# Float64 weights converted two tiles at a time, with larger shared homes and a new order of steps

## The chip, the cores and the metric

The kernel runs on one core of one Trainium2 chip. The metric is device time in microseconds (us) for one launch; lower is better.

## The reference, cut to what matters

Two attentions through a small "pack" of 32 tokens for each of 8 batches and 8 heads, and then a feed-forward layer over all 4608 tokens. The weights `w_in` and `w_out` come in float64, everything else in float32.

```python
def sm_attn(qq, kk, vv):
    s = scale * np.matmul(qq, kk.transpose(0, 1, 3, 2))
    s = s - np.max(s, axis=-1, keepdims=True)
    a = np.exp(s)
    a = a / (np.sum(a, axis=-1, keepdims=True) + 1e-09)
    return np.matmul(a, vv)
p_packed = sm_attn(p, k, v)                 # 32 packed tokens a head
out = sm_attn(q, p_packed, p_packed)        # (8, 8, 576, 64)
x = out.transpose(0, 2, 1, 3).reshape(4608, 512)
h = x @ w_in                                # 512 -> 2048
g = np.maximum(h, 0.0) + alpha * np.minimum(h, 0.0)
y = g @ w_out                               # 2048 -> 512
```

## The kernel before

Everything up to `h` is folded: for each batch the packed tokens are multiplied with `w_in` (tiles `pw`), and `first(k, f)` makes one 128 x 288 piece of `h` from `pw` and the attention weights `a` of half a batch `k` and the block `f` of 128 hidden columns. It then forms `neg`, `ps_h`, `gh` and `gl` on ScalarE (ACT) and VectorE (DVE): `g` split into a high and a low part. `second(k, f)` multiplies these with the block `f` of `w_out` (twelve matmuls, lines 693 to 695) into four accumulators. `order` lists the (k, f) pairs; I call one entry a step. Step i's `first` is issued together with step i-2's `second`. Batches 0 and 1 go in sweeps over a few blocks f at a time, so that a step needs only what has been converted by then; from batch 2 on all 16 blocks go in one sweep.

Before a weight can be used its float64 words are turned into float32 words on the chip by `convert`: DMA of the raw 64-bit words into `wraw`; ACT takes the magnitude of the high words (line 121, read with a step of two words) and scales the low words by 2^-29 (line 123); DVE clamps (125), shifts and masks (128), puts the sign back (132, whose first source is again every second word of `wraw`), and adds the low word as an exact 32-bit addition on 16-bit limbs (137 for `w_in`, 139 for `w_out`; shown in rows as CUSTOM_DVE or ISA, with twice the element count since the elements are 16-bit). For `w_out` ACT then rounds to the high part (141) and DVE subtracts it (142). One call converts one tile of 128 x 512; there are 16 tiles of `w_in` and 16 of `w_out`, and so 32 calls. `w_in` is also written back to DRAM (`w_whole`) for later batches.

The homes of `w_out` (tags `wo0` to `wo15`, 4 KB a partition each) serve as landing places before their own block is there: for the first k, v and q tiles, for the packed tokens `pt0`, and, five of them in turn (`SPARE`), for the raw words.

The order of the work is set in two ways. A fixed string, `'zzzzzzzzPzzzzozPzzoz'`, interleaves the attention of batch 0 (z), the conversions of the first block of `w_in` (P, `packed_w_fine`) and of `w_out` (o). After it a table of numbers, `plan`, says from which step on, and how often a step, each generator is advanced. The scheduler of the framework then sets the final order on each engine; every engine works through its own queue in that order, and SP is the queue that issues nearly all DMAs.

Of the kernel before, what the change touches and what calls it, by code (L numbers as in the profile page):

```python
# [28 lines left out]
def pack_attention_ffn_kernel(  # L29
# [54 lines left out]

    s1f = const.tile([P, NP, 2, 64], F32, name="s1f")
    ptf = const.tile([P, NP, 2, 64], F32, name="ptf")
    pt0 = const.tile([P, NP, 2, 64], F32, name="pt0", tag=f"wo{NF - 1}")
# [4 lines left out]
    s1 = const.tile([P, NP, 2, 64], F32R, name="s1")  # L92
    p2 = const.tile([P, NP, 2, 64], F32R, name="p2")
# [4 lines left out]
    nc.gpsimd.tensor_copy(out=ii[64:128], in_=ident[64:128, 64:128])  # L98
    for t in (ptf, pt0, fv(s1), fv(p2)):
        nc.gpsimd.memset(t, 0.0)  # L100
    wo_t = {}


    XF = 1

    def convert(src, raw, place, whole=None, room=None):
# [32 lines left out]
        nc.vector.tensor_tensor(out=bits, in0=bits, in1=low, op=ALU.add)  # L139
        hi, lo = place()  # L140
        nc.scalar.copy(out=hi, in_=mag)
        nc.vector.tensor_tensor(out=lo, in0=mag, in1=fv(hi), op=ALU.subtract)

    def new_raw(f=0):

        if f in left:
            left.remove(f)
            n = f
        elif f == NF - 1:
            n = f  # L150
        else:
            n = left.pop(0)
            left.append(n)
        return const.tile([P, 512], U64, name=f"wraw{n}", tag=f"wo{n}")

    SPARE = 5
    left = list(range(NF - 1 - SPARE, NF - 1))

    def convert_w_out(f):
        def place():  # L160
            wo_t[f] = const.tile([P, 2, DM], F32R, name=f"wo{f}", tag=f"wo{f}")
            return wo_t[f][:, 0, :], wo_t[f][:, 1, :]

        return convert(w_out[f * P : (f + 1) * P, :], new_raw(f), place)


    def load_x(src, b, pr):
        if b == 0 and (src is kT or pr == NP - 1):
            n = pr if src is kT else 2 * NP
            raw = const.tile([P, S], F32, name=f"xraw{n}", tag=f"wo{n}")  # L170
# [12 lines left out]
    def load_v(b, pr):  # L183
        if b == 0:
            raw = const.tile([P, KT, P], F32, name=f"vraw{pr}", tag=f"wo{NP + pr}")
# [43 lines left out]
    def attention(b, tp, exact=False):  # L229
# [6 lines left out]
        ts = slice(2 * tp, 2 * tp + 2)  # L236
        st1 = [s1f[:, pr, pr % 2] for pr in range(NP)] if exact else [s1[:, pr] for pr in range(NP)]
        st2 = [ptf[:, pr, b % 2] if exact else p2[:, pr] for pr in range(NP)]
# [7 lines left out]
        k1 = load_x(kT, b, pr1)  # L246
        yield
        if tp == 0:
            for r in range(2):
# [88 lines left out]
        yield  # L338
        c = sm.tile([P, 2, P], F32, name="c", tag="c", bufs=2)

        def pack(i, vs):
# [150 lines left out]
    def new_w32():  # L492
        return win.tile([P, 512], F32, name="w32", tag="w")

    def convert_w_in(j, pr, place, whole=None):
        src = w_in[pr * P : (pr + 1) * P, j * 512 : (j + 1) * 512]
        return convert(src, new_raw(), place, whole)

    def packed_w_fine(j):


        def get(f):
            cols = slice((4 * j + f) * P, (4 * j + f) * P + P)
# [18 lines left out]
        for f in range(4):  # L522
            ps = ps_m.tile([P, 512], F32, name="ps_m", tag="m")
            for pr in range(NP):
# [11 lines left out]
            if f == 3:  # L536
                done.update(("w", 0, j, pr) for pr in range(NP))
            if f < 2:
                ws.append(get(f + 2))
            yield  # L540

    def packed_w_first(j):

        ws = []
        for pr in range(NP):
            w = new_w32()
            drain(convert_w_in(j, pr, None, lambda: w))
            nc.sync.dma_start(out=w_whole[j, pr], in_=w)
            ws.append(w)
            if pr < 2:  # L550
                yield
                continue
            if pr == 2:
                gen = packed_w_whole(j, ws)
                next(gen)
                next(gen)
                yield
                continue
            next(gen)
            next(gen)  # L560
            yield

    def packed_w_two(bs, units, fresh):


        def get(j, pr):
            w = new_w32()
            if fresh:
                drain(convert_w_in(j, pr, None, lambda: w))
                nc.sync.dma_start(out=w_whole[j, pr], in_=w)  # L570
            else:
                nc.sync.dma_start(out=w, in_=w_whole[j, pr])
            return w

        for got in ahead(get, units):
            if got is None:
                yield
                continue
            (j, pr), w = got
            if pr == 0:  # L580
# [61 lines left out]
    def first(k, f):  # L642
# [132 lines left out]
    wf = packed_w_fine(0)  # L775
    wo = w_out_steps(range(NF))
# [8 lines left out]
    A2 = (24, 28, 35, 38, 50)  # L785
    AG = (0, 5, 11, 15, 24)
    plan = [(0, wf, 1), (WO[0], slower(WO[1], WO[2], wo), 1), (W1, packed_w_first(1), 1)]
    plan += [(0, gen, -2) for gen in later]
    plan += [(AT1[0], attention(1, 0, True), AT1[2]), (AT1[1], attention(1, 1, True), AT1[2])]
# [56 lines left out]
```

## Time and profile before

| | us |
|---|---|
| median of 3 runs (lowest, highest) | 795.83 (794.82, 796.27) |
| the profiled execution | 795.78 |
| its span, first to last instruction | 793.9 |
| outside the span | 1.9 |
| PE busy | 768.2 (97%) |
| ACT busy | 544.4 (69%) |
| DVE busy | 478.2 (60%) |
| POOL busy | 348.3 (44%) |

PE is TensorE's matmuls, PEld its weight loads. A busy share is a mean over the whole span; the kernel has a head, in which weights are converted and the first attentions run, and a long even part after it, and the shares differ between them. In rows with a time in front the first number is the start in us from the span's start, the second the duration. Durations of neighbouring instructions of one engine overlap a little, so the cost of one to its queue is the distance between two starts.

### The profile page before, as it was taken

How to read it: one execution, taken by the hardware profiler on the slowest of the kernel's cores; microseconds unless marked ns; L12 is line 12 of the kernel's file. 1: busy time of each engine (PE TensorE's matmuls, PEld its weight loads, DVE VectorE, ACT ScalarE, POOL GpSimd, SP SyncE). 2: the span in 40 equal slices, each digit the busy share in tenths (PEclk: the TensorE clock that was granted, in tenths of full speed). 3: DMA queues.
4: the chain of work that ended last, by engine and by line, in shares of the span. 5: the costliest groups of instructions: out<-in, count | busy, mean ns of one | idle time of the engine just before them, and what ended most of it. 6: DMA issues, size and time to landing. Idle time of an engine off the chain costs nothing.

```text
span 793.9 us, 15186 instructions
## 1 busy us (share of the span) xinstructions
PE 768.2 (97%) x5360; PEld 724.8 (91%) x5360; DVE 478.2 (60%) x1080; ACT 544.4 (69%) x1260; POOL 348.3 (44%) x327
## 2 busy tenths in 40 slices
PE   5699998999999999999999999999999999999997
PEld 4467677999899899999999999999999999999997
DVE  3999889678766335758565345757663344444443
ACT  5778789776667986767667876768678644444443
POOL 2102305654566764666664335667543222222220
PEclk9999999999999999999999999999999999999999
DMA  9887653211443981312223651222037000000000
GB/s 332 309 273 257 212 181 124 79 53 53 155 128 105 315 300 49 109 46 76 63 78 128 230 170 46 76 68 70 1 98 248 30 31 2 31 1 31 5 26 31
DMA packets 59611, 91.69 MB, mean 115 GB/s; under 512 B 5264, under 2 KB 37008, under 8 KB 59536
## 3 DMA queue, kind: packets, MB, share of 16 engines
q1 hardware_dynamic: 59248, 90.66, 35.1%
q8 instruction: 42, 0.69, 0.3%
q14 instruction: 33, 0.27, 0.1%
q10 hardware_dynamic: 288, 0.07, 0.0%
HBM read 68.69 MB, written 22.02 MB: 114 GB/s over the span
## 4 chain that ended last, share of the span: by engine, by line
PE 85%; DVE 5%; ACT 4%; DMA 4%; issue 1%; POOL 0%; SPq 0%; ACTq 0%; DVEq 0%
PE acc L693 16%; PE acc L694 16%; PE acc L695 16%; PE ps_h L663 7%; PE ps_h L665 7%; PE ps_h L664 7%; PE ps_h L651 3%; PE ps_m L350 2%; PE ps_m L587 2%; PE ps_m L216 1%; PE ps_m L217 1%; PE ps_m L622 1%; PE ps_m L624 1%; PE ps_m L623 1%; DMA w_whole<-w 1%
## 5 line engine op out<-in xcount | busy, mean ns | idle before, releaser
L693 PE MATMUL acc<-gh,wo 128*128 128x288 f32 x1024 | 287.2, 300 | 1.6 <-ACT gh L675 1.5
L694 PE MATMUL acc<-gh,wo 128*128 128x288 f32 x1024 | 282.5, 295 | 0.0
L639 POOL TENSOR_TENSOR pwl<-pw,pwh 128x512 fp32r<-128x512 f32 x112 | 146.4, 1308 | 218.7 <-ACT pwh L638 187.1
L670 DVE SCALAR_TENSOR_TENSOR ps_h<-neg,nal,ps_h 128x288 f32<-128x288 f32 x256 | 132.6, 519 | 151.6 <-ACT neg L669 150.9
L693 PEld LDWEIGHTS acc<-gh,wo 128*128 128x128 f32 x1024 | 192.2, 188 | 9.6 <-ACT gh L675 6.0
L695 PE MATMUL acc<-gl,wo 128*128 128x288 f32 x1024 | 199.4, 298 | 0.0
L694 PEld LDWEIGHTS acc<-gh,wo 128*128 128x128 f32 x1024 | 192.3, 188 | 1.9 <-issue 0.7
L676 DVE TENSOR_TENSOR gl<-ps_h,gh 128x288 fp32r<-128x288 f32 x256 | 116.2, 455 | 88.7 <-ACT gh L675 85.9
L695 PEld LDWEIGHTS acc<-gl,wo 128*128 128x128 f32 x1024 | 157.5, 188 | 4.2 <-issue 1.6
L675 ACT CAST gh<-ps_h 128x288 fp32r<-128x288 f32 x256 | 101.9, 400 | 72.9 <-DVE ps_h L670 70.8
L669 ACT ACTIVATE neg<-ps_h 128x288 f32<-128x288 f32 x256 | 104.8, 409 | 49.2 <-PE ps_h L665 39.0
L663 PE MATMUL ps_h<-a_h,pwh 128*128 128x288 f32 x448 | 133.4, 298 | 0.6 <-DVE gl L676 0.6
L665 PE MATMUL ps_h<-a_h,pwl 128*128 128x288 f32 x448 | 132.2, 295 | 0.0
L664 PE MATMUL ps_h<-a_l,pwh 128*128 128x288 f32 x448 | 132.2, 295 | 0.0
L638 ACT CAST pwh<-pw 128x512 fp32r<-128x512 f32 x112 | 69.4, 620 | 57.9 <-PE ps_h L664 56.1
L180 POOL TENSOR_TENSOR xl<-xraw,xh 128x576 fp32r<-128x576 f32 x48 | 69.8, 1455 | 71.8 <-ACT xh L179 67.8
L663 PEld LDWEIGHTS ps_h<-a_h,pwh 128*128 128x128 f32 x448 | 84.1, 188 | 1.6 <-DVE gl L676 1.1
L664 PEld LDWEIGHTS ps_h<-a_l,pwh 128*128 128x128 f32 x448 | 84.2, 188 | 1.0 <-issue 0.5
L665 PEld LDWEIGHTS ps_h<-a_h,pwl 128*128 128x128 f32 x448 | 84.1, 188 | 0.2
L627 ACT COPY pw<-ps_m 64x512 f32<-64x512 f32 x96 | 55.8, 581 | 5.8 <-PE ps_m L624 4.2
L309 POOL TENSOR_TENSOR vs<-vraw,vs 128x640 fp32r<-128x640 f32 x24 | 37.7, 1571 | 24.2 <-ACT vs L308 22.2
L219 ACT COPY lo<-ps_m 64x288 f32<-64x288 f32 x96 | 37.6, 396 | 10.1 <-PE ps_m L217 8.5
(130 smaller groups left out, 990.7 us busy)
## 6 DMA issues: line engine op xcount, KB each, us to landing
w<-w_split SPq DMA_DIRECT2D x32, 512.0 KB, 4.0
xraw<-in_kT SPq DMA_DIRECT2D x32, 288.0 KB, 3.0
xraw<-in_qT SPq DMA_DIRECT2D x32, 288.0 KB, 3.0
outT<-ot SPq DMA_DIRECT2D x64, 144.0 KB, 2.0
vraw<-in_v SPq DMA_DIRECT2D x32, 256.0 KB, 2.9
wraw<-in_w_in SPq DMA_DIRECT2D x16, 512.0 KB, 5.0
wraw<-in_w_out SPq DMA_DIRECT2D x16, 512.0 KB, 4.9
w_split<-w SPq DMA_DIRECT2D x16, 512.0 KB, 3.5
```

What stands on the lines that cost most here:

```text
L180: nc.gpsimd.tensor_tensor(out=xl, in0=raw, in1=fv(xh), op=ALU.subtract)
L639: nc.gpsimd.tensor_tensor(out=tl, in0=src, in1=fv(th), op=ALU.subtract)
L663: nc.tensor.matmul(ps[:, :HS], th[:, i, fs], a_h[:, i, tok], start=hi, stop=False)
L664: nc.tensor.matmul(ps[:, :HS], th[:, i, fs], a_l[:, i, tok], start=False, stop=False)
L665: nc.tensor.matmul(ps[:, :HS], tl[:, i, fs], a_h[:, i, tok], start=False, stop=lo)
L669: nc.scalar.activation(out=neg, in_=x, func=AF.Relu, scale=-1.0)
L670: nc.vector.scalar_tensor_tensor(out=x, in0=neg, scalar=nal[:, f : f + 1], in1=x, op0=ALU.mult, op1=ALU.add)
L675: nc.scalar.copy(out=gh, in_=x)
L676: nc.vector.tensor_tensor(out=gl, in0=x, in1=fv(gh), op=ALU.subtract)
L693: nc.tensor.matmul(acc[o][:, :HS], wo_t[f][:, 0, os_], gh, start=begin, stop=False)
L694: nc.tensor.matmul(acc[o][:, :HS], wo_t[f][:, 1, os_], gh, start=False, stop=False)
L695: nc.tensor.matmul(acc[o][:, :HS], wo_t[f][:, 0, os_], gl, start=False, stop=end)
```

## The change

Each call of `convert` now handles two tiles, 128 x 1024. The four (for `w_out` five) DVE instructions and the two (three) ACT instructions of a call have twice the width, and there are 16 calls in place of 32. For `w_in` the magnitude is made directly in the result tile `w32` (now 128 x 1024, four KB) and for `w_out` in one `mag` buffer of its own. The low word is scaled in place in `wraw`, so the exact addition reads it there, in every second 32-bit word, where it was read before from a dense tile `low`. Homes of `w_out` hold two blocks (8 KB, eight tags), three of them serve in turn for raw words. `c`, `ct` have one buffer, `gh` and `gl` two in place of three, and `s1` takes over the place of `s1f` once that is no longer read. The string and the table are new.

```diff
@@ convert
-        nc.sync.dma_start(out=raw if room is None else room, in_=src)
+        nc.sync.dma_start(out=raw.rearrange("p (r c) -> p r c", r=shape), in_=src)
...
-        mag = xin.tile([P, 512], F32, name="mag", tag="xh")
+        mag = whole if whole is not None else xin.tile([P, 1024], F32, name="mag", tag="mag", bufs=1)
...
-        low = xin.tile([P, 512], U32, name="low", tag="xl")
-        nc.scalar.activation(out=low, in_=u[:, :, 0], func=AF.Copy, scale=2.0**-29)
+        low = u[:, :, 0]
+        nc.scalar.activation(out=low, in_=low, func=AF.Copy, scale=2.0**-29)
...
+        nc.vector.tensor_tensor(out=bits, in0=bits, in1=low, op=ALU.add)
         if whole is not None:
-            nc.vector.tensor_tensor(out=whole().bitcast(U32), in0=bits, in1=low, op=ALU.add)
             return
...
-    SPARE = 5
-    left = list(range(NF - 1 - SPARE, NF - 1))
+    SPARE = 3
+    left = list(range(NF // 2 - 1 - SPARE, NF // 2 - 1))
...
-        gh = gp.tile([P, HS], F32R, name="gh", tag="gh", bufs=3)
-        gl = gp.tile([P, HS], F32R, name="gl", tag="gl", bufs=3)
+        gh = gp.tile([P, HS], F32R, name="gh", tag="gh", bufs=2)
+        gl = gp.tile([P, HS], F32R, name="gl", tag="gl", bufs=2)
...
-    for ch in 'zzzzzzzzPzzzzozPzzoz':
+    for ch in 'zzzzzzzzPPzzzozzzzoz':
...
-    WO, W1, AT1 = (-5, 5, 4), 0, (0, 2, -6)
-    PW1, PW01, PW01B = (9, -2), (13, 3), (24, -8)
+    WO, W1, AT1 = (0, 1, 8), 3, (1, 2, -5)
+    PW1, PW01, PW01B = (9, 1), (15, 1), (24, -11)
```

In the new kernel line 129 is the load of raw words, 135 and 137 are the two ACT passes, 139, 142, 146 and 150 the four DVE passes, 155 and 156 the split of `w_out`; 664 is `first` of batch 0, 683 and 689 are what 670 and 676 were, and 706 to 708 are `second`.

The first place is SP's queue at the start, where the loads of batch 0 (q as `xraw`, v as `vraw`) stand among the raw words of `w_in` and `w_out`. Before:

```order
L173 DMA xraw<-in_qT 128x576
L115 DMA wraw_199<-in_w_in 128x4x128
L173 DMA xraw<-in_qT 128x576
L189 DMA vraw_234<-in_v 128x4x128
L193 DMA vraw_234<-in_v 64x128
L173 DMA xraw<-in_qT 128x576
L173 DMA xraw_269<-in_qT 128x576
L115 DMA wraw_271<-in_w_out 128x512
```

and now:

```order
L189 DMA xraw<-in_qT 128x576
L129 DMA wraw_193<-in_w_in 128x4x256
L129 DMA wraw_203<-in_w_in 128x4x256
L189 DMA xraw<-in_qT 128x576
L205 DMA xraw_170<-in_v 128x4x128
L209 DMA xraw_170<-in_v 64x128
L189 DMA xraw<-in_qT 128x576
L129 DMA wraw_258<-in_w_out 128x2x512
```

The whole first quarter of `w_in` (two loads of 1 MB) now stands ahead of the second q tile, where one load of 512 KB stood.

The second place is DVE's queue just ahead of step 0, whose line is 670 before and 683 now. Before:

```order
L125 TENSOR_SCALAR mag<-mag 128x512
L432 STREAM_TRANSPOSE a_f<-t_346 128x288
L125 TENSOR_SCALAR mag<-mag 128x512
L128 TENSOR_SCALAR mag<-mag 128x512
L137 ISA w_478<-mag,low 128x1024
L128 TENSOR_SCALAR mag<-mag 128x512
L132 SCALAR_TENSOR_TENSOR mag<-wraw_522,mag 128x512
L670 SCALAR_TENSOR_TENSOR ps_h<-neg,nal,ps_h 128x288 x2
```

and now:

```order
L146 SCALAR_TENSOR_TENSOR mag<-wraw_315,mag 128x1024
L452 STREAM_TRANSPOSE a_f<-t_332 128x288
L447 RECIPROCAL z_334<-z_334 128x9
L319 TENSOR_SCALAR den<-den 128x1
L150 ISA mag<-wraw_315,mag 128x2048
L448 TENSOR_TENSOR t_332<-t_332,z_334 128x288
L320 RECIPROCAL den<-den 128x1
L139 TENSOR_SCALAR w_528<-w_528 128x1024
L452 STREAM_TRANSPOSE a_f<-t_332 128x288
L683 SCALAR_TENSOR_TENSOR ps_h<-neg,nal,ps_h 128x288
```

Up to this place the old queue has added the low words of 9 tiles and begun two more; the new one has added those of 4 pairs, 8 tiles, and begun a fifth pair.

The third place is PE's queue ahead of the first `second` (line 693, now 706). Before:

```order
L373 MATMUL ps_m<-ident,c 128x64 x2
L527 MATMUL ps_m<-w_367,pt_103 128x128 x4
L651 MATMUL ps_h<-a_f,pw 128x288 x2
L487 MATMUL ps_m<-w_379,pt_103 128x512
L212 MATMUL ps_m<-xraw,ptf 64x288
L487 MATMUL ps_m<-w_478,pt_103 128x512
L212 MATMUL ps_m<-xraw,ptf 64x288
L693 MATMUL acc_656<-gh,wo_281 128x288
```

and now:

```order
L550 MATMUL ps_m<-w_202,pt_103 128x128 x4
L348 MATMUL ps_m<-ident,s_t 128x128 x5
L664 MATMUL ps_h<-a_f,pw 128x288 x2
L365 MATMUL ps_m<-vraw,aT 128x128 x5
L228 MATMUL ps_m<-xraw,s1f 64x288
L706 MATMUL acc_506<-gh,wo_267 128x288
```

Two matmuls of the second quarter of `w_in` (line 487), the end of the second pack and a score matmul that stood ahead of step 0's `second` now come behind it.

## Rows read from the trace of the kernel before

**Rows 1.** The page's busy times, and its picture of the span in 40 slices of 19.8 us (busy tenths; PEclk is TensorE's granted clock in tenths of full speed).

```profile
PE 768.2 (97%) x5360; PEld 724.8 (91%) x5360; DVE 478.2 (60%) x1080; ACT 544.4 (69%) x1260; POOL 348.3 (44%) x327
PE   5699998999999999999999999999999999999997
...
DVE  3999889678766335758565345757663344444443
ACT  5778789776667986767667876768678644444443
...
PEclk9999999999999999999999999999999999999999
```

**Rows 2.** Busy time by stage: the stretch, its length, then busy us and instructions of PE, PEld, DVE, ACT and POOL, the granted clock, the DMA share and GB/s.

```profile
0.00:40.00 40.00, 24.71 (x123) 18.92 (x124) 27.55 (x77) 25.84 (x70) 8.74 (x25) 0.96 0.93 320
40.00:60.00 20.00, 19.55 (x96) 13.66 (x95) 19.74 (x44) 16.09 (x36) 1.59 (x3) 0.91 0.83 268
60.00:80.00 20.00, 18.67 (x112) 15.11 (x112) 19.96 (x40) 17.04 (x41) 4.90 (x6) 1.00 0.81 259
80.00:100.00 20.00, 20.00 (x92) 12.61 (x90) 15.97 (x32) 15.29 (x35) 6.55 (x5) 1.00 0.65 212
100.00:120.00 20.00, 19.93 (x100) 14.34 (x100) 17.56 (x38) 17.69 (x35) 0.00 (x0) 1.00 0.57 184
120.00:140.00 20.00, 18.01 (x117) 15.52 (x116) 18.66 (x39) 18.13 (x40) 11.62 (x7) 1.00 0.36 114
...
300.00:800.00 500.00, 489.48 (x3639) 484.81 (x3637) 259.56 (x584) 312.10 (x727) 215.77 (x191) 1.00 0.22 69
```

**Rows 3.** Groups of DVE instructions between 0 and 160 us: line, operation, output and input, shapes, count, busy us, mean ns of one, idle time before them.

```profile
L132 DVE SCALAR_TENSOR_TENSOR mag<-wraw,mag 128x512 uint32<-128x512 uint32 x30 | 22.2, 741 | 0.1
...
L125 DVE TENSOR_SCALAR mag<-mag 128x512 f32<-128x512 f32 x30 | 12.7, 423 | 3.9 <-ACT mag L121 3.7
L142 DVE TENSOR_TENSOR wo<-mag,wo 128x512 fp32r<-128x512 f32 x14 | 11.9, 849 | 0.0
L137 DVE CUSTOM_DVE_ANT_0 w<-mag,low 128x1024 uint16<-128x1024 uint16 x16 | 11.5, 719 | 0.8 <-PE ps_m L587 0.6
```

**Rows 4.** DVE in order of time, a stretch without a pause (start, duration, line).

```profile
22.59 0.68 DVE L137 CUSTOM_DVE_ANT_0 w<-mag,low 128x1024 uint16<-128x1024 uint16 x1
23.18 0.69 DVE L142 TENSOR_TENSOR wo<-mag,wo 128x512 fp32r<-128x512 f32 x1
23.79 0.42 DVE L128 TENSOR_SCALAR mag<-mag 128x512 uint32<-128x512 uint32 x1
24.12 0.45 DVE L419 TENSOR_REDUCE m<-t 128x9 f32<-128x288 f32 x1
24.48 0.45 DVE L420 TENSOR_TENSOR t<-t,m 128x288 f32<-128x288 f32 x1
24.85 0.42 DVE L125 TENSOR_SCALAR mag<-mag 128x512 f32<-128x512 f32 x1
25.19 0.69 DVE L132 SCALAR_TENSOR_TENSOR mag<-wraw,mag 128x512 uint32<-128x512 uint32 x1
25.79 0.45 DVE L420 TENSOR_TENSOR t<-t,m 128x288 f32<-128x288 f32 x1
```

**Rows 5.** DVE in order of time: the first pass of the first three conversions, and step 0 (in brackets the pause before and what ended it).

```profile
12.39 0.43 DVE L125 TENSOR_SCALAR mag<-mag 128x512 f32<-128x512 f32 x1
...
17.21 0.43 DVE L125 TENSOR_SCALAR mag<-mag 128x512 f32<-128x512 f32 x1 [1.91 <-ACT mag L121]
...
19.28 0.43 DVE L125 TENSOR_SCALAR mag<-mag 128x512 f32<-128x512 f32 x1 [0.46 <-ACT mag L121]
...
47.66 0.94 DVE L670 SCALAR_TENSOR_TENSOR ps_h<-neg,nal,ps_h 128x288 f32<-128x288 f32 x2
```

**Rows 6.** ACT in order of time, three instructions without a pause.

```profile
28.10 0.62 ACT L141 CAST wo<-mag 128x512 fp32r<-128x512 f32 x1
28.62 0.66 ACT L123 ACTIVATE low<-wraw 128x512 uint32<-128x512 uint32 x1
29.19 0.67 ACT L213 COPY s_t<-ps_m 64x288 f32<-64x288 f32 x2
```

**Rows 7.** PE in order of time: a wait of the head, the two matmuls of line 487 ahead of step 0's `second`, and that `second`.

```profile
37.34 1.33 PE L328 MATMUL ps_m<-ident,s_t 128*128 128x128 f32 x5 [5.38 <-ACT s_t L294]
...
46.89 1.02 PE L487 MATMUL ps_m<-w,pt 128*128 128x512 f32 x2
...
48.47 1.12 PE L487 MATMUL ps_m<-w,pt 128*128 128x512 f32 x2
...
50.15 0.41 PE L693 MATMUL acc<-gh,wo 128*128 128x288 f32 x1
```

**Rows 8.** All engines in order of time in the even part: the last matmul of one step's `first`, the `gl` matmuls of the step two before it, then `gh` and `gl` of the step itself.

```profile
687.72 0.30 PE L665 MATMUL ps_h<-a_h,pwl 128*128 128x288 f32 x1
687.85 0.70 PE L695 MATMUL acc<-gl,wo 128*128 128x288 f32 x4
...
689.11 0.40 ACT L675 CAST gh<-ps_h 128x288 fp32r<-128x288 f32 x1 [0.59 <-DVE ps_h L670]
...
689.54 0.46 DVE L676 TENSOR_TENSOR gl<-ps_h,gh 128x288 fp32r<-128x288 f32 x1 [0.47 <-ACT gh L675]
```

**Rows 9.** The chain that ended last, in order of time: its piece for the first raw words (start, us).

```profile
7.18 4.49 DMA wraw<-in_w_in
```

More of the change, by code (lines that the diff above doesn't have):

```diff
@@ L98, in pack_attention_ffn_kernel, with s1_late, room, convert @@
     nc.gpsimd.tensor_copy(out=ii[64:128], in_=ident[64:128, 64:128])
-    for t in (ptf, pt0, fv(s1), fv(p2)):
+    for t in (ptf, pt0, fv(p2)):
         nc.gpsimd.memset(t, 0.0)
-    wo_t = {}
+    wo_t, first_raw, late = {}, {}, {}
+    def s1_late():
+        if not late:
+            late[0] = const.tile([P, NP, 2, 64], F32R, name="s1", tag="s1")
+            nc.gpsimd.memset(fv(late[0]), 0.0)
+        return late[0]
+    def room(n, size):
+        slot, at_ = {0: (0, 0), 1: (0, 1), 2: (0, 2), 3: (1, 0), "v0": (1, 1), "v1": (1, 2),
+                     "v2": (2, 0), "v3": (2, 1), "q": (2, 2)}[n]
+        if slot not in first_raw:
+            first_raw[slot] = const.tile([P, 3, KT * P], F32, name=f"xraw{slot}", tag=f"wo{slot}")
+        return first_raw[slot][:, at_, :size]
     XF = 1
-    def convert(src, raw, place, whole=None, room=None):
-        nc.sync.dma_start(out=raw if room is None else room, in_=src)
+    def convert(src, raw, shape, place, whole=None):
+        nc.sync.dma_start(out=raw.rearrange("p (r c) -> p r c", r=shape), in_=src)
         yield
@@ L135, in convert @@
         )
+        nc.vector.tensor_tensor(out=bits, in0=bits, in1=low, op=ALU.add)
         if whole is not None:
[L137 removed]
             return
[L139 removed]
         hi, lo = place()
[L141 to L142 removed]
+        two = mag.rearrange("p (r c) -> p r c", r=2)
+        nc.scalar.copy(out=hi, in_=two)
+        nc.vector.tensor_tensor(out=lo, in0=two, in1=fv(hi), op=ALU.subtract)
     def new_raw(f=0):
@@ L153, in new_raw @@
             left.append(n)
-        return const.tile([P, 512], U64, name=f"wraw{n}", tag=f"wo{n}")
-    SPARE = 5
-    left = list(range(NF - 1 - SPARE, NF - 1))
+        return const.tile([P, 1024], U64, name=f"wraw{n}", tag=f"wo{n}")
+    SPARE = 3
+    left = list(range(NF // 2 - 1 - SPARE, NF // 2 - 1))
     def convert_w_out(f):
         def place():
-            wo_t[f] = const.tile([P, 2, DM], F32R, name=f"wo{f}", tag=f"wo{f}")
-            return wo_t[f][:, 0, :], wo_t[f][:, 1, :]
-        return convert(w_out[f * P : (f + 1) * P, :], new_raw(f), place)
+            two = const.tile([P, 2, 2, DM], F32R, name=f"wo{f}", tag=f"wo{f}")
+            for i in range(2):
+                wo_t[2 * f + i] = two[:, i]
+            return two[:, :, 0, :], two[:, :, 1, :]
+        src = w_out[2 * f * P : (2 * f + 2) * P, :].rearrange("(r p) c -> p r c", p=P)
+        return convert(src, new_raw(f), 2, place)
     def load_x(src, b, pr):
         if b == 0 and (src is kT or pr == NP - 1):
-            n = pr if src is kT else 2 * NP
-            raw = const.tile([P, S], F32, name=f"xraw{n}", tag=f"wo{n}")
+            raw = room(pr if src is kT else "q", S)
         else:
@@ L184, in load_v @@
         if b == 0:
-            raw = const.tile([P, KT, P], F32, name=f"vraw{pr}", tag=f"wo{NP + pr}")
+            raw = room(f"v{pr}", KT * P).rearrange("p (kt d) -> p kt d", d=P)
         else:
@@ L236, in attention @@
         ts = slice(2 * tp, 2 * tp + 2)
-        st1 = [s1f[:, pr, pr % 2] for pr in range(NP)] if exact else [s1[:, pr] for pr in range(NP)]
+        if exact:
+            st1 = [s1f[:, pr, pr % 2] for pr in range(NP)]
         st2 = [ptf[:, pr, b % 2] if exact else p2[:, pr] for pr in range(NP)]
@@ L247, in attention @@
         yield
+        if not exact:
+            s1 = s1_late()
+            st1 = [s1[:, pr] for pr in range(NP)]
         if tp == 0:
@@ L544, in packed_w_first, with packed_w_two, get @@
         ws = []
[L545 to L550, printed above, removed]
+        for two in range(NP // 2):
+            ws += convert_w_in(j, two)
+            yield
+        for _ in packed_w_whole(j, ws):
+            yield
+    def packed_w_two(bs, units, fresh):
+        got = {}
+        def get(j, pr):
+            if pr % 2 == 0:
+                if fresh:
+                    ws = convert_w_in(j, pr // 2)
+                else:
+                    w = new_w32().rearrange("p (r c) -> p r c", r=2)
+                    nc.sync.dma_start(out=w, in_=w_whole[j, pr : pr + 2].rearrange("r p c -> p r c"))
+                    ws = w[:, 0, :], w[:, 1, :]
+                got.update({(j, pr): ws[0], (j, pr + 1): ws[1]})
+            return got[j, pr]
+        for step in ahead(get, units):
+            if step is None:
                 yield
                 continue
[L553 to L579, printed above, removed]
+            (j, pr), w = step
             if pr == 0:
```

52 lines of the change are left out of this document (25 added, 27 removed).

## The prediction, as put on record before the changed kernel ran

> **What bounds the kernel now.** I read the page's busy times first, then busy time by stage, then DVE, ACT and PE in order of time in the head. PE is busy 97% of the span, and from 300 us on it is never short of work except at the very end; there DVE and ACT are busy half to two thirds of the time [rows 1, 2]. Nothing in the change alters how many matmuls PE runs, so what can be won is time in which PE stands without work, and that lies in the head: 15.3 us of the first 40, and 0.5, 1.3, 0, 0.1 and 2.0 us in the next five stretches of 20, together 19.1 us up to 140 us [rows 2]. In the same stretches DVE is the fullest engine: 19.7 and 20.0 of 20 us between 40 and 80, then 16.0, 17.6 and 18.7, with ACT at 15 to 18 [rows 2]. The DMA engines are 93% busy up to 40 us and fall off after 80 us [rows 2]. So up to about 80 us the pace is that of DVE's queue, whose largest part is the conversion of weights; up to 140 us DVE and ACT share that role; after that it is PE's.
>
> **The price of a conversion on DVE.** In a stretch without a pause, starts are 0.59 to 0.61 us apart behind the passes of lines 137, 142 and 132, 0.33 and 0.34 us behind those of lines 128 and 125, and 0.36 and 0.37 us behind softmax passes of width 288 [rows 4]. Widths 288 and 512 give 0.235 us for 224 columns, 1.05 ns a column, and a fixed 0.06 us; the two clamping and masking passes run at twice that rate with the same fixed part. A tile of `w_in` thus costs 0.34 + 0.33 + 0.60 + 0.60 = 1.87 us, a tile of `w_out` 0.61 more, 2.48. At width 1024 the passes come to 0.60, 0.60, 1.14 and 1.14 us: 3.48 us for a pair of `w_in` where two tiles cost 3.74, and 4.62 against 4.96 for `w_out`. Eight pairs of each: 8 x 0.26 + 8 x 0.34 = **4.8 us less on DVE**.
>
> **The addition that now reads every second word.** That sum takes the addition at 1.14 us. No row shows it with such a source. The nearest is line 132, a two-source pass that also takes every second word of `wraw`: 0.60 us, no more than the dense line 142 at 0.61 [rows 4], and over the whole head it is the shorter of the two, 741 ns against 849 in the mean [rows 3]. From below, then, the step costs nothing. From above: the addition handles 1024 limbs in the 0.59 us in which other passes handle 512 words [rows 4], so two limbs at a time; if the gaps between words made it take limbs one by one, it would need 1.05 ns x 2048 + 0.06 = 2.2 us, 1.07 us more, and 16 x 1.07 = 17 us in all. I take the lower end, by the row that has the same step, and keep the upper one as a rival.
>
> [...]
>
> **ACT.** Forty fewer instructions. The dense pass of line 141 takes 0.52 us of the queue, the one that reads every second word 0.57 [rows 6]; with a fixed part like DVE's they save 40 x 0.06 = 2.4 us. The low word is now also written with a step: if that costs as much as reading so does (0.05 us for 512), 16 x 0.1 = 1.6 us are given back. I take 1 us less on ACT, not on the path before 80 us. If a stepped write halved ACT's rate, each pass would take 1 us more, 16 us together, in stretches where ACT has 2 to 5 us free in 20 [rows 2]; no row speaks for it.
>
> **The start.** Raw words now come 1 MB at a time. The first 512 KB took 4.49 us from 7.18 [rows 9]; another 512 KB at the 320 GB/s of this stretch [rows 2] is 1.6 us, and ACT's first pass is 0.5 us longer, so DVE begins its first conversion at about 14.6 in place of 12.39. Against that, the old queue then paused 1.91 and 0.46 us for its second and third tile [rows 5]; the new one has a pair, 3.48 us of work, while the next 1 MB (3.3 us) arrives, and I give it 0.7 us of pauses. SP also issues both loads ahead of the second q tile, so that the scores behind it come a microsecond later; DVE has conversions to do meanwhile. Net **+0.5 us**.
>
> **Step 0.** Ahead of it the old queue holds 6 tiles of `w_in`, 3 of `w_out` and 1.9 us of two begun ones: 11.2 + 7.4 + 1.9 = 20.5 us. The new one holds two pairs of `w_in`, one of `w_out`, one of `w_out` without its last pass, and one clamp: 7.0 + 4.6 + 3.5 + 0.6 = 15.7 us. So line 683 should run near 47.66 - 4.9 + 0.5 = 43.3 us [rows 5], and the first `second` near 46 in place of 50.15 [rows 7]. This is mostly order, not gain: PE has then yet to do the two matmuls of the second quarter (about 1.9 us) and some eight small ones (at most 0.27 us each, by the five in 1.33 us) that stood ahead [rows 7]. The gain that lasts is DVE's saving, which the full engine passes on to PE between 20 and 140 us.
>
> **Edits costed at nothing.** Two buffers for `gh` and `gl`: a new `gl` must wait for the `gl` matmuls two steps back. In the even part those start at 687.85 and are over by 688.6, and the `gl` that would take the place starts at 689.54 [rows 8]: 0.9 us of cover in each step. Without it DVE, and the next `first` behind it, would wait. One buffer for `c`, `ct` and `mag`: ACT waits for a DVE pass at most, about 0.4 us for `c` and one conversion for `mag`, hidden as long as ACT has those 2 to 5 us. `s1` in the place of `s1f` adds one short memset between two ACT instructions. Smaller room for raw words (three pairs for five tiles) makes SP wait for DVE, as it does now. The new step numbers move work within the head; I set them at 0, with 4 us either way, about a fifth of PE's 19.1 us.
>
> **The sum.** -4.8 + 0.5 = -4.3 us. The profiled execution took 795.78 (span 793.9 and 1.9 outside), 0.05 under the median: 795.8 - 4.3 = **791.5 us**. A change under 0.2%, 1.6 us, I count as none, being about what three runs of this kernel can tell apart.
>
> **Rivals.**
> *The saving is hidden* (0.15). DVE is full but PE still waits for something else in the head: ACT's exponential for 5.38 us before 37.34 [rows 7], or DMA at 93%. For it: the first 20 us hang on transfers, and the bytes are the same. Against it: that wait for ACT itself stands behind DVE's passes, and DVE has no pause from 20 to 80 us. Time: 795.8 - 4.8 + 0.5 + the loss of about 3 to 5 from coarser steps, 794.5 to 796.5.
> *The stepped addition is slow* (0.09; slower than before). Place: line 150. It decides from 4.3 / 16 = 0.27 us extra an addition; at the full 1.07 us the 17 us, less the 3 us or so that DVE has free between 80 and 140 in excess of what it needs, give 795.8 - 4.3 + 14 = 805; at half of it, 798. [...]
> *The coarser order costs more than DVE saves* (0.08; slower). Passes of 1.14 us stand ahead of the short ones that PE waits for: each step of the head has two (lines 683, 689), and half a pass more ahead of each in 16 steps would be 16 x 2 x 0.27 = 9 us if PE had no work ahead, of which I would expect a good half to show: 797 to 799.
> *The new order also removes PE's waits* (0.08). Up to half of the 15.3 us idle before 40 us cannot go, since data must come first; but 4 us more than the sum is possible: 785 to 787.
>
> **How the numbers follow.** The forecast's own case has 0.60, with 787 to 794 as its range; the case above adds 0.08: faster 0.68. No change 0.15. Slower 0.09 + 0.08 = 0.17. The range 786.5 to 798.5 leaves out most of the slow addition and of the best case, under 0.2 together, and holds the slow ends of the middle ones.
>
> **What would show it.** Right: line 150 near 1.2 us in duration (1.14 apart), DVE's conversion lines down by about 5 us in all, the first 706 before 47 us, DVE still full up to some 75 us, PE's idle time to 140 us near 15 us, and the even part unchanged at the same pace. Wrong: line 150 at 2 us or more; ACT's line 137 well over 1.1 us; waits of `gl` for line 708 in the even part; or DVE with pauses before 60 us that end with a DMA.

## The result, and the profile after

The changed kernel is slower: 800.58 us (median of 5 runs, 797.78 to 801.35) against 795.40 (794.82 to 796.27). The ratio is 1.0058, 95% interval 1.0039 to 1.0078. The profiled execution took 800.58 us with a span of 798.8, 4.9 more than before. The prediction said 791.5, and 786.5 to 798.5 as its range.

The page after, as in [rows 1]:

```profile
PE 768.2 (96%) x5360; PEld 723.8 (91%) x5360; DVE 479.5 (60%) x1008; ACT 541.8 (68%) x1220; POOL 354.6 (44%) x327
PE   5798999899999999999999999999999999999997
DVE  3998777967877335577665266776553344444443
ACT  4778778776776986777668867777576644444443
PEclk9999999999999999999999999999999999999999
```

PE does the same work; VectorE (DVE) is not less busy, GpSimd (POOL) 6.3 us more. Busy time by stage, in the columns of [rows 2]:

```profile
0.00:40.00 40.00, 25.69 (x127) 19.28 (x128) 26.74 (x63) 24.52 (x58) 6.33 (x22) 0.99 0.94 330
40.00:60.00 20.00, 18.42 (x101) 14.29 (x100) 18.46 (x30) 15.16 (x30) 2.83 (x5) 0.93 0.79 246
60.00:80.00 20.00, 17.29 (x109) 14.48 (x109) 17.37 (x26) 16.46 (x36) 8.22 (x8) 1.00 0.71 247
80.00:100.00 20.00, 18.21 (x65) 9.04 (x63) 14.21 (x18) 15.07 (x30) 8.70 (x7) 1.00 0.56 191
100.00:120.00 20.00, 20.00 (x95) 13.89 (x95) 15.89 (x27) 15.77 (x27) 2.58 (x2) 1.00 0.59 192
120.00:140.00 20.00, 18.06 (x118) 15.72 (x116) 14.31 (x25) 16.61 (x32) 8.08 (x5) 1.00 0.39 141
140.00:160.00 20.00, 17.18 (x123) 16.09 (x123) 20.00 (x33) 15.58 (x34) 9.89 (x7) 1.00 0.12 33
300.00:800.00 500.00, 494.07 (x3671) 488.53 (x3669) 265.96 (x589) 315.39 (x736) 219.20 (x193) 1.00 0.23 72
```

Up to 40 us PE gets 1 us more done than before, and from 300 us on nothing has changed (idle for 4.7 us up to the span's end, against 4.4). The loss lies between 40 and 160 us: PE is busy for 109.2 us there, against 116.0. And DVE, which was full up to 80 us, now has pauses: 80.2 us of 100 between 40 and 140, against 91.9. Then it is full, 20.00 of 20, in a stretch in which it had 11.88 us to do before:

```profile
140.00:160.00 20.00, 19.82 (x152) 19.59 (x151) 11.88 (x29) 15.03 (x40) 13.66 (x15) 1.00 0.28 78
```

Three places stand out. Here is the first, in order of time on each engine (start, duration; idle time before it and what ended that in brackets):

```profile
78.92 1.41 POOL L477 TENSOR_TENSOR a_l<-s,a_h 128x576 fp32r<-128x576 f32 x1 [0.71 <-ACT a_h L476]
80.28 2.39 POOL L196 TENSOR_TENSOR xl<-xraw,xh 128x576 fp32r<-128x576 f32 x1
...
79.06 2.34 DVE L146 SCALAR_TENSOR_TENSOR mag<-wraw,mag 128x1024 uint32<-128x1024 uint32 x1
81.44 2.31 DVE L150 CUSTOM_DVE_ANT_0 mag<-wraw,mag 128x2048 uint16<-128x2048 uint16 x1
...
83.84 1.04 ACT L155 CAST wo<-mag 128x1024 fp32r<-128x1024 f32 x1 [2.32 <-DVE mag L150]
84.90 0.39 ACT L229 COPY s<-ps_m 64x288 f32<-64x288 f32 x1
...
85.35 1.98 PE L507 MATMUL ps_m<-w,pt 128*128 128x512 f32 x4 [1.79 <-ACT s L229]
```

As I read it, DVE and GpSimd take turns. L146 takes 1.22 us in the median; here it takes 2.34, of which 1.07 lie behind the end of L477 at 80.33. L196 takes 1.41 when it runs again at 86.07 and 2.39 here, 1.27 of it behind the end of L146 at 81.40. L150, also 1.22 in the median, takes 2.31, 1.08 of it behind the end of L196 at 82.67. Behind it ScalarE (ACT) stands 2.32 us at the split L155, behind L155 the score copy L229, and behind that PE. The block of `w_out` that is converted here is first needed near 180 us, 100 us later. The second place is one chain of DVE passes from 132 to 157 us, three `w_out` pairs with the softmax of batch 2 between them; its end:

```profile
152.76 1.89 DVE L146 SCALAR_TENSOR_TENSOR mag<-wraw,mag 128x1024 uint32<-128x1024 uint32 x1
154.77 2.39 DVE L150 CUSTOM_DVE_ANT_0 mag<-wraw,mag 128x2048 uint16<-128x2048 uint16 x1
...
154.12 1.96 POOL L329 TENSOR_TENSOR vs<-vraw,vs 128x640 fp32r<-128x640 f32 x1 [0.56 <-ACT vs L328]
156.09 2.35 POOL L196 TENSOR_TENSOR xl<-xraw,xh 128x576 fp32r<-128x576 f32 x1
```

And ACT now waits for raw words. Of its waits between 40 and 160 us (total, times, longest), these are for loads of weights, 8.5 us together; before there was none in this stretch:

```profile
ACT wraw L137 <- DMA wraw<-in_w_in: 4.8, 3, 2.7
ACT mag L135 <- DMA wraw<-in_w_out: 1.8, 2, 1.2
ACT wraw L137 <- DMA wraw<-in_w_out: 1.1, 1, 1.1
ACT w L135 <- DMA wraw<-in_w_in: 0.8, 1, 0.8
```

A load of 1 MB of `w_out` takes 8.2 us from issue to landing in this stretch, one of 512 KB took 4.8 before. The longest of these waits makes the third place, earlier than the other two:

```profile
56.40 1.17 ACT L137 ACTIVATE wraw<-wraw 128x1024 uint32<-128x1024 uint32 x1 [2.75 <-DMA wraw<-in_w_in]
...
58.22 1.19 PE L228 MATMUL ps_m<-xraw,ptf 128*64 128x288 f32 x4 [0.99 <-ACT ptf L402]
60.77 0.70 PE L228 MATMUL ps_m<-xraw,ptf 128*64 128x288 f32 x2 [1.37 <-ACT s L229]
```

The copies L402 and L229, for which PE waits here, stand in ACT's queue behind this late L137; ACT has no pause from there on until 61 us. The two waits are 2.4 us of the 10.8 for which PE is idle between 40 and 160 us; before, it was 4.0.

### The profile page after: what moved, and what is told of

It is laid out like the page before. It is cut to its first block, busy times and chain, and to the rows that moved or that the text cites. A ratio compares the mean times of both kernels' runs of the same rounds, so it can differ in the third digit from the quotient of the medians.

```text
span 798.8 us, 15095 instructions
## 1 busy us (share of the span) xinstructions
PE 768.2 (96%) x5360; PEld 723.8 (91%) x5360; DVE 479.5 (60%) x1008; ACT 541.8 (68%) x1220; POOL 354.6 (44%) x327
## 4 chain that ended last, share of the span: by engine, by line
PE 84%; DVE 7%; ACT 4%; DMA 3%; issue 1%; POOL 0%; ACTq 0%; DVEq 0%
PE acc L706 16%; PE acc L707 16%; PE acc L708 15%; PE ps_h L676 7%; PE ps_h L677 7%; PE ps_h L678 7%; PE ps_h L664 3%; PE ps_m L600 2%; PE ps_m L370 2%; PE ps_m L232 2%; PE ps_m L233 2%; DMA xraw<-in_kT 1%; PE ps_m L635 1%; DVE mag L150 1%; PE acc L223 1%
## 5 line engine op out<-in xcount | busy, mean ns | idle before, releaser
L706 PE MATMUL acc<-gh,wo 128*128 128x288 f32 x1024 | 286.6, 300 | 2.2 <-ACT gh L688 2.1
L652 POOL TENSOR_TENSOR pwl<-pw,pwh 128x512 fp32r<-128x512 f32 x112 | 149.3, 1334 | 248.6 <-ACT pwh L651 206.5
L683 DVE SCALAR_TENSOR_TENSOR ps_h<-neg,nal,ps_h 128x288 f32<-128x288 f32 x256 | 132.7, 518 | 151.1 <-ACT neg L682 149.9
L706 PEld LDWEIGHTS acc<-gh,wo 128*128 128x128 f32 x1024 | 192.2, 188 | 8.9 <-ACT gh L688 4.3
L196 POOL TENSOR_TENSOR xl<-xraw,xh 128x576 fp32r<-128x576 f32 x48 | 71.6, 1492 | 49.8 <-ACT xh L195 49.8
L329 POOL TENSOR_TENSOR vs<-vraw,vs 128x640 fp32r<-128x640 f32 x24 | 38.1, 1589 | 19.3 <-ACT vs L328 19.1
```

The lines of the kernel that those rows point to most:

```text
L196: nc.gpsimd.tensor_tensor(out=xl, in0=raw, in1=fv(xh), op=ALU.subtract)
L652: nc.gpsimd.tensor_tensor(out=tl, in0=src, in1=fv(th), op=ALU.subtract)
L683: nc.vector.scalar_tensor_tensor(out=x, in0=neg, scalar=nal[:, f : f + 1], in1=x, op0=ALU.mult, op1=ALU.add)
L706: nc.tensor.matmul(acc[o][:, :HS], wo_t[f][:, 0, os_], gh, start=begin, stop=False)
```

## The experiments

The theories, with the letters that the expectations use. **O**: the new string and table put the work in worse places. **W**: wide passes hold up what stands behind them, above all where they and GpSimd wait for each other. **D**: raw words come late, 1 MB at a time into three places. **B**: the smaller buffers. Differences below are differences of the ratios to the kernel before, taken of 795.4 us; that of the changed kernel is +4.6 us. By the intervals of the two ratios, a difference between two runs is good to some 1.8 us either way, and a smaller one is not shown by the time alone.

### Exchanging the orders

```diff
-    WO, W1, AT1 = (0, 1, 8), 3, (1, 2, -5)
-    PW1, PW01, PW01B = (9, 1), (15, 1), (24, -11)
+    WO, W1, AT1 = (0, 1, 8), 0, (0, 2, -6)
+    PW1, PW01, PW01B = (9, -2), (13, 3), (24, -8)
```

with the other numbers and the string alike, in the changed kernel:

> The changed kernel with the string and the step numbers of the kernel before (only the spacing of w_out, which is now counted in pairs, stays). Theory W (width): the loss comes from passes of 1.2 us on VectorE, which stand ahead of short ones and stretch to 2.3 us beside GpSimd; the order does not matter much, so 799 to 802 us. Theory O (order): the new string and table put conversions and GpSimd's subtractions into the same stretches (77 to 90 us and 130 to 160 us); with the old numbers both places vanish: 789 to 795 us. Theory B (buffers: one mag, two gh and gl, one c, three places for raw words): the buffers are unchanged here, 799 to 802 us.

811.9 us, ratio 1.0204 (1.0186 to 1.0223). The reverse, the kernel before with the new numbers:

> The kernel before with the string and the step numbers of the changed one; two tiles of w_out are converted where the changed kernel converts a pair. All passes stay 512 wide, all buffers as before. Theory W: 793 to 797 us, as before. Theory O: 798 to 802 us, the loss goes along with the numbers. Theory B: 793 to 797 us.

808.97 us, 1.0169 (1.0153 to 1.0185). Both are worse than either kernel, which no theory expected, so they decide nothing: the scheduler lays out every queue anew, and the same numbers give other queues. The next two met the same end. First, each DVE pass of a conversion in two halves; shown is the addition:

```diff
+        halves = [slice(0, 512), slice(512, 1024)]
...
+        for h in halves:
+            nc.vector.tensor_tensor(out=bits[:, h], in0=bits[:, h], in1=low[:, h], op=ALU.add)
```

> The changed kernel, but each VectorE pass of a conversion is issued as two passes 512 wide (loads, ScalarE passes, buffers and step numbers stay as changed). This gives back the 4.8 us that wider passes save on VectorE. Theory W: short passes get between the halves and a stretched one holds up half as much, 794 to 798 us. Theories O and B: nothing is gained and VectorE has 4 to 5 us more to do, 800 to 804 us.

807.08 us, 1.0147 (1.0130 to 1.0164). Second, two buffers for `mag`:

```diff
-name="mag", tag="mag", bufs=1
+name="mag", tag="mag", bufs=2
-tc.tile_pool(name="op", bufs=4)
+tc.tile_pool(name="op", bufs=2)
```

> The changed kernel with two buffers for mag; the room comes from the output staging ot (two buffers in place of four), used only in the last step of each half batch. Theory B: ScalarE no longer waits for the last pass of the pair ahead, 796 to 798 us. Theories W and O: 799 to 802 us.

822.71 us, 1.0335 (1.0319 to 1.0352). Nothing can be read from a part that is changed while the order changes with it. So from here on I held the order: each instruction gets an edge, for its place in the queue alone, on the one ahead of it in the queue of its base kernel, on all five engines:

```python
for ahead, behind in zip(queue, queue[1:]):
    tc.add_manual_dep(behind, ahead.name, DependencyInfo(NoSync, DATA))
```

In the traces of runs that change only the number of buffers or landing places (`before_small_buffers`, `fixed_raw4`), ACT, DVE, GpSimd and SP have their instructions in the order of the base kernel. The two buffers for `mag` in the held order:

> The changed kernel in its own order with two buffers for mag (the room comes from ot, two buffers in place of four). The trace shows 0.7 us of ScalarE waiting for the single buffer between 40 and 160 us: 800 to 801 us, or up to 1 us less. Theory B: 797 to 798.5 us.

859.67 us, 1.0809 (1.0775 to 1.0844), which is the price of the room I took. PE's waits from 160 to 800 us:

```profile
PE acc L706 <- DVE ot L722: 17.5, 10, 3.7
PE acc L706 <- DVE ot L716: 9.1, 4, 3.2
PE acc L706 <- ACT ot L720: 7.9, 7, 1.3
```

Two buffers of `ot` are too few; what a second `mag` is worth stays open.

### DVE's saving, and the small buffers

The halves of `new_halves`, now next to each other in the held order:

> The changed kernel in its own order, each VectorE pass of a conversion issued as two passes 512 wide that stand next to each other, so that nothing but their fixed cost (some 4.8 us in all) comes back. If VectorE's saving reaches the end, as predicted: 804 to 806 us. If it is hidden: 800 to 801 us. Theory W (length of one pass, when GpSimd has to wait for its end or it for GpSimd's): 797 to 799 us.

804.31 us, 1.0117 (1.0103 to 1.0131): 4.7 us over the changed kernel, the size of what I said DVE saves. It is not a clean measure of that, and theory W's figure missed too: many halves took longer than alone, which I put down to GpSimd, since two that stand together can both be held up. The group of the sign pass for `w_out` (1.22 us whole in the median; a half of `w_in` has 686 ns in the mean) shows the longer halves (busy, mean ns):

```profile
L150 DVE SCALAR_TENSOR_TENSOR mag<-wraw,mag 128x512 uint32<-128x512 uint32 x16 | 15.0, 981 | 0.0
```

So something of DVE's time reaches the end; how much of the 4.7 us is fixed cost stays open.

The kernel before, in its own order:

```diff
-name="gh", tag="gh", bufs=3
+name="gh", tag="gh", bufs=2
-name="gl", tag="gl", bufs=3
+name="gl", tag="gl", bufs=2
-name="c", tag="c", bufs=2
+name="c", tag="c", bufs=1
-name="ct", tag="ct", bufs=2
+name="ct", tag="ct", bufs=1
```

> The kernel before, in its own order on every engine, with two buffers for gh and gl and one for c and ct, as in the changed kernel. As predicted (these cost nothing): 795 to 796 us. Theory B (the smaller buffers are the loss): 797 to 800 us.

795.10 us, 0.9995 (0.9986 to 1.0004): nothing, as predicted.

### Contention

```diff
-        nc.gpsimd.tensor_tensor(out=xl, in0=raw, in1=fv(xh), op=ALU.subtract)
+        nc.gpsimd.memset(fv(xl), 0.0)
```

and likewise for `vs`, `a_l`, `pwl`; both kernels in their own order.

> The changed kernel in its own order, leaving out part of the computation: GpSimd's subtractions that make the low parts (xl, vs, a_l, pwl) are replaced by setting these tiles to zero. Theory W (VectorE's wide passes and GpSimd's subtractions hold each other up): passes of 2.3 us go back to 1.2 us, 794 to 797 us, a gain clearly larger than the same edit gives in the kernel before. If contention does not matter, or does as much before: the same gain in both, 798 to 800 us here.

794.38 us, 0.9988 (0.9979 to 0.9996).

> The kernel before in its own order with the same edit, leaving out the same part. Theory W: a gain of at most 1.5 us, 794 to 795.5 us. Rival: the same gain as in the changed kernel.

792.65 us, 0.9969 (0.9957 to 0.9981). The changed kernel gains 5.6 us, the one before 2.5. The difference, 3.1 us and good to some 2, is the best figure here for the contention that the change added; without the subtractions 1.5 us of loss are left. PE's idle time between 40 and 160 us falls from 10.8 to 6.2 us in the changed kernel, and only from 4.0 to 3.7 in the one before. The edit also makes GpSimd's own work shorter (184.1 us busy in place of 354.6), so that places may come free earlier for SP's loads; this was not separated. What speaks for contention is that the long passes are gone. DVE's groups (busy, mean ns), the changed kernel first:

```profile
L150 DVE CUSTOM_DVE_ANT_0 mag<-wraw,mag 128x2048 uint16<-128x2048 uint16 x8 | 12.3, 1542 | 0.0
L146 DVE SCALAR_TENSOR_TENSOR mag<-wraw,mag 128x1024 uint32<-128x1024 uint32 x8 | 11.5, 1438 | 0.0
```

and without the subtractions:

```profile
L146 DVE SCALAR_TENSOR_TENSOR mag<-wraw,mag 128x1024 uint32<-128x1024 uint32 x8 | 9.7, 1216 | 0.0
L150 DVE CUSTOM_DVE_ANT_0 mag<-wraw,mag 128x2048 uint16<-128x2048 uint16 x8 | 9.7, 1215 | 0.0
```

The chain of the first place there:

```profile
77.69 1.23 DVE L146 SCALAR_TENSOR_TENSOR mag<-wraw,mag 128x1024 uint32<-128x1024 uint32 x1
78.95 1.22 DVE L150 CUSTOM_DVE_ANT_0 mag<-wraw,mag 128x2048 uint16<-128x2048 uint16 x1
```

and a pass that does meet a memset:

```profile
131.94 1.21 DVE L150 CUSTOM_DVE_ANT_0 mag<-wraw,mag 128x2048 uint16<-128x2048 uint16 x1
...
132.42 0.58 POOL L196 MEMSET xl<- 128x576 f32 x1 [3.23 <-PE ps_m L233]
```

The passes were longer beside the subtractions before the change too: L142 has 828 ns in the mean in the kernel before, and 759 without them. What all instructions took above the median of their groups, added up from 40 to 160 us, is an estimate of the time held up, from the traces: on DVE 8.3 us before, 9.7 in the changed kernel and 11.9 with its halves (`fixed_halves`); on GpSimd 2.7, 9.5 and 4.9. So what grew with the width of the passes is above all the time for which GpSimd waits. DVE's own loss is hardly larger than before; in the first place it falls on a chain for which PE waits.

Can it be had without leaving work out? Two subtractions later, and on SP's queue two loads of q that wait for them:

```diff
@@ GpSimd's queue, from 80 us
-L196 TENSOR_TENSOR xl<-xraw,xh 128x576 x2
 L463 TENSOR_TENSOR t<-t,m 128x576
...
 L652 TENSOR_TENSOR pwl<-pw,pwh 128x512
+L196 TENSOR_TENSOR xl<-xraw,xh 128x576
 L652 TENSOR_TENSOR pwl<-pw,pwh 128x512
+L196 TENSOR_TENSOR xl<-xraw,xh 128x576
```

> The changed kernel in its own order, but for two of GpSimd's subtractions (xl of batch 2, at 80.28 and 86.07 us, first read after 126 us), which go behind its first and second pwl subtraction (99 us and later, where GpSimd pauses), and two loads of q on SyncE that wait for them, which go behind the write of w_whole near 107 us. Theory W: VectorE's addition at 81.44 us takes 1.2 in place of 2.3 us and the split and score copy behind it come a microsecond earlier, 798.5 to 800 us. Otherwise 800 to 802 us.

801.45 us, 1.0067 (1.0052 to 1.0083), no gain. L150 and step 8's L683 (90.47 in the changed kernel) show that the place mended in part (L146 there still took 2.47 us), and ACT's row that the moved loads made the raw words behind them late:

```profile
80.35 1.23 DVE L150 CUSTOM_DVE_ANT_0 mag<-wraw,mag 128x2048 uint16<-128x2048 uint16 x1
88.29 0.52 DVE L683 SCALAR_TENSOR_TENSOR ps_h<-neg,nal,ps_h 128x288 f32<-128x288 f32 x1
...
114.99 1.12 ACT L135 ACTIVATE w<-wraw 128x1024 f32<-128x1024 f32 x1 [4.07 <-DMA wraw<-in_w_in]
```

### Places in the queues

The five DVE passes and the ACT split of the pair with blocks 8 and 9 later, on DVE from 77 us to the pauses between 101 and 129 us:

```diff
@@ DVE's queue
-L139 TENSOR_SCALAR mag<-mag 128x1024
 L689 TENSOR_TENSOR gl<-ps_h,gh 128x288
-L142 TENSOR_SCALAR mag<-mag 128x1024
-L146 SCALAR_TENSOR_TENSOR mag<-wraw_1045,mag 128x1024
-L150 ISA mag<-wraw_1045,mag 128x2048
-L156 TENSOR_TENSOR wo_1054<-mag,wo_1054 128x2x512
...
 L689 TENSOR_TENSOR gl<-ps_h,gh 128x288
+L139 TENSOR_SCALAR mag<-mag 128x1024
+L142 TENSOR_SCALAR mag<-mag 128x1024
```

> Every engine's queue is held in exactly the order it has in the changed kernel, except that one conversion, that of the w_out pair with blocks 8 and 9 (VectorE passes between 76.7 and 86.1 us, first used after 180 us), is moved: its five VectorE passes go into pauses between 101 and 129 us, its ScalarE split behind the scaling of the low words at 123 us. Theory O (a place in the queue, nothing else: the split stands in front of the score copy for which PE waits, and the conversion is 100 us early): 796 to 798 us, PE's loss between 75 and 90 us shrinks by 2.5 to 4.5 us. Theory W (passes of 1.2 us, stretched beside GpSimd, hold up the short ones wherever they stand): the loss moves along, 799 to 801 us.

800.74 us, 1.0072 (1.0058 to 1.0086), no gain. The same for the last two pairs, one pass a step behind the `gl` of steps 28 to 40:

> As the run before, but the pair with blocks 8 and 9 stays where it was and the last two w_out pairs (blocks 12 to 15, VectorE passes between 141 and 160 us, first used after 200 us) are moved: one pass a step behind the gl of steps 28 to 40 (160 to 200 us), their ScalarE passes likewise. Theory O: VectorE is no longer full between 140 and 160 us, the chain of VectorE alone from 132 to 157 us goes, 795 to 797 us. Theory W: the loss moves into 160 to 200 us, 799 to 801 us.

802.59 us, 1.0091 (1.0077 to 1.0105), 2.6 us worse. Both moves:

> Both moves of the two runs before together. Theory O: the gains add, 791 to 794 us, under the kernel before. Theory W: 799 to 801 us.

802.45 us, 1.0094 (1.0078 to 1.0109). The two places did mend (between 140 and 160 us no DVE chain is left), but the passes then stood elsewhere in the way. In the last run PE waits for DVE at the ends of sweeps, where the partial sums (L716) must free the accumulators:

```profile
189.08 0.41 PE L706 MATMUL acc<-gh,wo 128*128 128x288 f32 x1 [1.00 <-DVE part L716]
203.63 0.37 PE L706 MATMUL acc<-gh,wo 128*128 128x288 f32 x1 [1.24 <-DVE part L716]
```

So a gentler move: only the split and its DVE subtraction at the first place, and the last two pairs spread clear of these ends.

```diff
@@ ACT's queue, from 83.8 us
-L155 CAST wo<-mag 128x1024
 L229 COPY s<-ps_m 64x288
 L195 CAST xh<-xraw 128x576
 L509 COPY pw<-ps_m 128x512
 L712 COPY part<-acc 128x288 x4
 L509 COPY pw<-ps_m 128x512
+L155 CAST wo<-mag 128x1024
```

> The changed kernel in its own order but for two moves. The ScalarE split of the w_out pair with blocks 8 and 9 goes behind the score copies and pw copies that stood behind it (83.84 us), its VectorE subtraction behind the next gl; the conversions of the last two w_out pairs are spread, one pass a step, over steps 22 to 33 (VectorE was full from 132 to 157 us), clear of the ends of the sweeps. Theory O (places in the queues): 795 to 797.5 us. Theory W, or a VectorE that is short of time everywhere: 800 to 803 us.

798.11 us, 1.0038 (1.0024 to 1.0052): 1.6 us better, where 3 to 5 were expected. (The traced execution took 800.37 us, the longest of the five.) The second place is gone and some of it comes back behind it, as PE's first number shows (17.18 and 40.00 in the changed kernel):

```profile
140.00:160.00 20.00, 19.77 (x151) 19.53 (x151) 14.41 (x29) 14.58 (x37) 11.05 (x9) 1.00 0.16 45
160.00:200.00 40.00, 39.05 (x249) 35.06 (x248) 32.21 (x74) 27.14 (x66) 21.53 (x21) 1.00 0.19 55
```

### Raw words

```diff
-    SPARE = 3
+    SPARE = 4
```

> The changed kernel in its own order on every engine, with four landing places of 1 MB for raw words in place of three (the fourth is the home of blocks 6 and 7, free until their own conversion). Theory D (raw words come late: ScalarE waits 8.5 us for them between 40 and 160 us, where it waits for none before, because a load of 1 MB takes 6 to 8 us and may start only when a whole pair is done with its place): loads on SyncE start earlier, 796 to 798.5 us. Theory W (width of the passes) and theory B (the other single buffers): 800 to 801 us.

798.18 us, 1.0037 (1.0024 to 1.0049), 1.7 us better. But ACT's waits for raw words, which theory D holds to be the loss, did not shrink: 9.1 us between 40 and 160 us, against 8.5. SP's longest wait for a place of raw words is gone; in the changed kernel it was

```profile
SPq L129 <- DVE mag L150: 6.1, 1, 6.1
```

Each load as two, with ACT's passes in halves behind them:

```diff
+        for h in range(2):
+            hs = slice(h * shape // 2, (h + 1) * shape // 2)
+            nc.sync.dma_start(out=to[:, hs], in_=src[:, hs])
```

> The changed kernel in its own order, every load of raw words issued as two loads of 512 KB, and each of the two ScalarE passes behind it as two passes 512 wide, so that the first may run while the second half arrives. Theory D (raw words come late because they come 1 MB at a time): the 8.5 us that ScalarE waits for raw words shrink to half, 797 to 799 us, though ScalarE gets 2 to 3 us more to do. If loads are late only for want of a free place: 800 to 802 us.

798.57 us, 1.0040 (1.0026 to 1.0055), 1.4 us better; ACT's waits for raw words fall from 8.5 to 6.2 us, not to half. Each of these three gains, of the moves, the fourth place and the halved loads, lies within what the intervals allow, so none is shown. Nor do they add up:

> The fourth landing place and the two moves together. If D and O both hold: 791.5 to 794.5 us, under the kernel before. If neither: 800 to 803 us.

797.96 us, 1.0035 (1.0023 to 1.0048), 1.8 us better in place of 3.3.

> The changed kernel with the fourth landing place, loads in halves, the two moves in the queues, and GpSimd's two subtractions later. If the four remedies act on different waits: 793 to 795.5 us, level with the kernel before or under it. If they act on the same waits, as the fourth place and the moves did: 796 to 798 us.

804.70 us, 1.0118 (1.0099 to 1.0136). This has the later GpSimd subtractions with their loads, and as in the run with those alone (3.1 us) PE waits for `pw`, here 3.3 us up to 118.6 us, behind ACT's wait for `w_in`. No version beat the kernel before.

## Why the prediction was wrong

**Right.** The stepped addition: L150 takes 1.22 us in the median, as L146 does, so the rival of a slow addition falls, though the time lies in its range (798 to 805). The price of a pair: the groups of the conversion lines add up to 78.1 us, before to 88.9; 72 fewer instructions overlap their neighbours by 0.08 us less (L142 in [rows 4]: 0.69 long, the next 0.61 behind its start), 5.8 us, and 5.0 are left, where I had 4.8. That undoing it costs 4.7 is partly luck, since the halves also took longer than alone. ACT's stepped write: 1.17 us a pass. Step 0: L683 at 42.84 (43.3 predicted), the first L706 at 44.69 (46). Buffers of `gh`, `gl`, `c`, `ct`: nothing. The even part: as before. In order of time, the changed kernel:

```profile
42.84 0.48 DVE L683 SCALAR_TENSOR_TENSOR ps_h<-neg,nal,ps_h 128x288 f32<-128x288 f32 x1
...
44.69 0.40 PE L706 MATMUL acc<-gh,wo 128*128 128x288 f32 x1
```

and ACT's group of that pass (busy, mean ns, idle before it and what ended that):

```profile
L137 ACT ACTIVATE wraw<-wraw 128x1024 uint32<-128x1024 uint32 x16 | 18.6, 1166 | 6.6 <-DMA wraw<-in_w_in 4.8 <-DMA wraw<-in_w_out 1.7
```

**The step that failed** is the part on edits costed at nothing, with the new step numbers. I set these at 0, 4 us either way. If the 4.7 us are saved, the rest of the change must cost some 9 us to come out at +4.6. Of this the runs and traces show three causes. Only the first is clear of the intervals, and only just; the other two are read from the traces:

- Contention with GpSimd, some 3.1 us more than before, good to 2. It was no term of the sum at all, though [rows 3] had L142 at 849 ns in the mean, far above its price, and I used that figure only to compare two lines. In the first place L146, L196 and L150 ended 1.07 to 1.27 us after the other engine's instruction that each had met: held up, as I read it, by what was left of that, and a pass of twice the width can leave more. L146 took 2.34 us there beside subtractions, and had 1.22 in the mean where the subtractions only set zeros.
- Raw words. "Makes SP wait for DVE, as it does now" was wrong: a place is held for a whole pair, up to its addition (SP waited up to 6.1 us for L150), and a load takes 8.2 us in place of 4.8. ACT waits 8.5 us where it waited for none, and in the third place this costs PE 2.4 us. That a remedy gives time back is not shown: 1.7 us for a fourth place, with ACT's waits as long as before, and 1.4 for halved loads.
- Places: conversions 40 to 100 us ahead of their use stand in front of work for which PE waits (1.79 us at L507 in the first place); two moves gave 1.6 us in the median, which is not shown either, and three other runs with moves gained nothing.

The last two overlap (1.8 us for the fourth place and the moves together), so they are no ledger. The reason behind the gain, "which the full engine passes on to PE", did not hold either: DVE was not the full engine any more (35.8 us busy between 40 and 80 us, before 39.7); it paused there for ACT, 3.8 us, and ACT for loads of weights, 3.8, and between 40 and 160 us 4.0 at the split L155 for L150. PE's idle time up to 140 us, 15 us by the prediction, was 22.3. What makes up the remaining 3 to 5 us of the 9 is open. The new numbers by themselves were not separated, nor was the single `mag`, for which the trace shows 0.7 us of ACT's time, nor the reading back of `w_in`, which also became two tiles a load.

**The rivals.** The nearest was the coarser order that costs more than DVE saves, 797 to 799 us at a chance of 0.08. Its mechanism, half a pass more ahead of each short one, is not what the rows show in the first place: there the passes take 2.34 and 2.31 us beside GpSimd, and the copy for which PE waits stands behind the second of them. But no run tests it: in the held order the halves stand next to each other, and in `new_halves` the order changed too. The new numbers taking waits away did not happen.

## What to carry to other kernels

Doubling the width of DVE's passes saved 5.0 us of its time here, by the groups of the traces, and was paid where another engine, a landing place or an in-order queue had to wait for a whole pass, load or pair (between 40 and 160 us ACT's split 4.0 us for L150, SP 6.1 for a place, ACT 8.5 for raw words). List for each which engine it holds up and is held up by, who waits for its place, and what stands behind it. A group whose mean lies well above its undisturbed duration, as L142 with 849 ns in [rows 3] and 0.69 us in [rows 4], is a term of the sum. Where a scheduler orders the queues, test one part in a held order, or the new order is measured in place of the edit.

## What the runs showed of the hardware

In the first place DVE's L146 and L150 and GpSimd's L196 met and ran nearly one after the other: 1.22 us became 2.34 and 2.31, and 1.41 became 2.39, in the same 5 us, while a pass L150 that met a memset in the run without subtractions took 1.21. The clamp L139, 0.69 us in the median, took 1.34 at 76.73, while L329 ran on GpSimd from 75.95 to 77.51; but in the run without subtractions its eight passes for `w_in` took 812 ns in the mean, against 689 in the changed kernel, and this was not explained. A pass that reads every second word of its second source took what a dense one took: 1.22 us in the median for L150, and 1.21 for the dense L156.
